# Later products with V, tiles of V grouped by head group, and the masked exponentials in two buffers (attention decode with a gated MLP, one core)

## The chip, the cores and the metric

The kernel runs on one core of a Trainium2 chip. The metric is the device time of one execution in microseconds (us). It is given as the median of several runs. Beside it there is one profiled execution, whose trace gives the start and the duration of every instruction and every DMA packet. All times of day in this text are us from the start of the profiled span.

## The reference

A decode step of eight sequences with one token each. Attention has 32 query heads and 8 key/value heads of 128, so four query heads share one key/value head, and it looks at the last 2048 positions of the cache:

```python
xn = layernorm(x)                                   # x: 8 x 1 x 512
q = (xn @ wq) split into 32 heads of 128
scores = q . k_cache[:, :, Sk-2048:] * 128**-0.5    # 8 kv heads
o = softmax(scores) @ v_cache[:, :, Sk-2048:]
s = o (8 x 4096) @ wo                               # -> 8 x 512
h = sigmoid(xn @ w_gate) * (xn @ w_up)              # 512 -> 1792
return x + s * silu(h @ w_down)
```

All inputs are bfloat16. What has to be read is the window of K (33.6 MB), the window of V (33.6 MB), `wq` and `wo` (4.2 MB each), and `w_gate`, `w_up` and `w_down` (1.8 MB each): 81.0 MB in all, all of it used once.

## The kernel before

**Tiles and rings.** All loads go through the queue of SyncE (SP), in one fixed order. `wq`, K and the three late weights share a ring of three buffers of 32 KB per partition (`KRING`); V has a ring of four buffers of 16 KB (`VRING`). K comes as eight tiles of 4.19 MB (K0 to K7), four for each *set* of four sequences; V as sixteen tiles of 2.10 MB (V0 to V15), one per sequence `b` and head group `gg` (four kv heads each), in the order of `divmod(i, NG)`: sequence after sequence, the two head groups of a sequence in turn. The order on the queue is `wq`, K0 to K6, V0, V1, K7, V2 to V13, `w_gate`, `w_up`, V14, V15, `w_down`, and `wo` in eight pieces.

**Slots.** The kernel is scheduled by hand: the loop at L651 runs over slots `t`, and each engine executes its instructions in the order in which the slots write them. A slot holds at most the following, in this order:

- L657 `soft_max_part`: a maximum on VectorE (DVE) over the scores of a K tile that is complete;
- L660 `soft_exp` at `EXP_AT` = 36 and 68: two small DVE instructions, then four Exp on ScalarE (ACT), L484, with the sum of each row;
- L663 `soft_mask`: four DVE instructions (L539) that multiply the transposed exponentials `pc_bf` of one head group with the four columns of a 0/1 mask, into `pT_sb`, the stationary operand of the products with V. `pT_sb` is one buffer for both head groups of a set (pool `work`, one buffer), and it is taken anew when `gg == 0`;
- L665 `k_turn(t)` for t < 64: a quarter of a half of a K tile is transposed in place on DVE (L441), eight of them per tile;
- L670 `soft_turn` (four DVE transposes, L504) one slot after `soft_exp`;
- L672 `qk(t - 4)`: four matmuls on TensorE (PE, L456) with what `k_turn(t - 4)` made;
- L674 `pv_sum`: once per V tile, the matmuls of L616 that add up a finished product, and the DVE scaling into `o_sb` (L625). They read `acc_sb`, which ACT copies out of PSUM (L606);
- L676 `pv(u)`: a quarter of a V tile's products (L595). After the fourth quarter ACT's copy L606 is written down;
- L679 `soft_spread` two slots after `soft_exp`: eight matmuls (L517) and four ACT casts (L525) that make `pc_bf`;
- L681 `soft_den`: the row sums and their reciprocals, on DVE, PE and DVE (L551 to L577).

**When a load is issued.** `issue_loads` (L198) issues the next load of the fixed order as soon as the buffer that it takes is free in the order of the program: K7 after `qk(39)` (slot 43) has let K4 go, V(i+4) after the fourth quarter of V(i). On the chip that is a wait of SP for the engine that read the buffer last. A load that waits holds up all those behind it on the queue.

**Where the products stand.** `PV_AT` says at which slot the products of a set begin: 49 for the first and 83 for the second (L64 to L67). V(i) of the first set has the slots 49 + 4i to 52 + 4i. `soft_mask` comes one or two slots ahead of `PV_AT`: slots 47 and 48, and 81 and 82. `soft_den` comes in slots 48 and 82. The products of the first set's tiles (`PV_WIDE`, i < 8) take four chunks of V per matmul, those of the second set two.

After the products come the MLP (L688 to L693, L696), the rearrangement of `o_sb` (L695), the product with `wo` (L702) and two small DVE instructions ahead of the store.

Of the kernel before, what the change touches and what calls it, by code (L numbers as in the profile page):

```python
# [10 lines left out]
def kernel(  # L11
# [14 lines left out]
    P = 128  # L26
# [3 lines left out]
    rep = Hq // Hkv  # L30
# [11 lines left out]
    GL = 4  # L42
    NG = Hkv // GL
    PP = P // GL
    CH = W // PP
    NQ = P // 32
    NJ = 4
    CC = CH // NJ
    NT = B * NG
    NSLOT = NT * NJ  # L50


    HB = B // NQ
# [7 lines left out]
    VSET = NT // HB  # L61
    QK_LAG = 4
    EXP_AT = [SET * (hb + 1) + QK_LAG for hb in range(HB)]
    PV_LAG = 13  # L64
    PV_AT = [EXP_AT[0] + PV_LAG]
    for hb in range(1, HB):
        PV_AT.append(max(EXP_AT[hb] + 5, PV_AT[hb - 1] + VSET * NJ + 2))  # L67


    NA = Dh // 64  # L70
    CB = CH // 2
# [6 lines left out]
    bf16 = mybir.dt.bfloat16  # L78
# [6 lines left out]

    consts = ctx.enter_context(tc.tile_pool(name="consts", bufs=1))
    work = ctx.enter_context(tc.tile_pool(name="work", bufs=1))
    small = ctx.enter_context(tc.tile_pool(name="small", bufs=2))
    kring = ctx.enter_context(tc.tile_pool(name="kring", bufs=KRING))
    vring = ctx.enter_context(tc.tile_pool(name="vring", bufs=VRING))  # L90
# [14 lines left out]
    def load(dst, src, q=None):  # L105
        if q is None:
            q = nc.sync
        q.dma_start(out=dst, in_=src)  # L108
# [4 lines left out]
    def v_tile(shape, name):  # L113
        return vring.tile(shape, bf16, name=name, tag="vring", align_bytes=ALIGN)
# [10 lines left out]
    def load_k(i):  # L125
# [8 lines left out]
        )  # L134
        k_tiles[i] = t

    def load_v(i):
        b, gg = divmod(i, NG)
        t = v_tile([P, CH, Dh], "v_sb")
        load(  # L140
            t[:].rearrange("p c d -> p (c d)"),
            A_v_cache[b, GL * gg : GL * (gg + 1), win0:Sk, :].rearrange(
                "j (p c) d -> p j (c d)", c=CH
            ),
        )
        v_tiles[i] = t
# [18 lines left out]
    def load_wo():  # L165
# [19 lines left out]
        (kind, i)  # L185
        for _, kind, i in sorted(
            [(KTS * i, 0, i) for i in range(NKT)]
            + [(NJ * (i % VSET) + PV_AT[i // VSET], 1, i) for i in range(NT)]
        )
    ]  # L190
    loads[-2:-2] = [(2, 0)]
# [6 lines left out]
    def issue_loads():  # L198
# [36 lines left out]
        out=rstd[:], in_=mv[:, 1:2], func=AF.Sqrt, bias=eps_t[:], scale=1.0  # L235
# [4 lines left out]
        out=xn_bf[:],  # L240
# [7 lines left out]
    for kt in range(KT):  # L248
        nc.tensor.transpose(
            out=xnT_ps[:, kt, :], in_=xn_bf[:B, kt::KT], identity=ident[:B, :B]  # L250
        )
    x2_ps = psum1.tile([NCOL * 32, DC], f32, name="x2_ps", tag="misc")
    for c in range(NCOL):
# [23 lines left out]
        out=PermF[:], in_=ident[:].rearrange("m (h q r) -> m q h r", q=NQ, r=rep)  # L277
# [4 lines left out]
        out=Hm[:],  # L282
# [7 lines left out]
    for j in range(GL):  # L290
        for gg in range(NG):
            g = NG * gg + j // 2
            nc.vector.tensor_copy(
                out=spread[:, gg, j % 2, :, j], in_=ident[:, 32 * g : 32 * g + PP]
# [3 lines left out]
    for w in (32, 64):  # L298
        rows_of = small.tile([P, w], f32, name=f"rows_of{w}")
        nc.vector.tensor_reduce(  # L300
            out=rows_of[:],
# [12 lines left out]
    for gg in range(NG):  # L314
        rows = slice(32 * gg, 32 * (gg + 1))
        cols = slice(NE * GL * rep * gg, NE * GL * rep * (gg + 1))
        for e in range(NE):
            nc.vector.tensor_copy(
                out=pick[rows, e, cols].rearrange("p (h d) -> p h d", d=NE)[:, :, e],
# [105 lines left out]
    pT_of = {}  # L425
# [7 lines left out]
    def k_turn(t):  # L433

        i, n = divmod(t, KTS)
        a, cq = divmod(n, 4)
        kw = k_tiles[i][:].rearrange("p c d -> p (c d)").bitcast(f32)
        kw = kw.rearrange("p (c a w) -> p c a w", a=NA, w=32)[
            :, KC4 * cq : KC4 * (cq + 1), a, :
        ]  # L440
        nc.vector.transpose(out=kw, in_=kw)  # L441
# [24 lines left out]
    def soft_max_part(i):  # L466
        hb, kq = divmod(i, NK)
        if kq == 0:
            mx_of[hb] = small.tile([P, NK], f32, name="mx")
        nc.vector.reduce_max(  # L470
            out=mx_of[hb][:, kq : kq + 1], in_=s_tiles[i][:], axis=AX.X
        )
# [24 lines left out]
    def soft_turn(hb):  # L497

        p_bf = p_of.pop(hb)[:].rearrange("p c k j o -> p (c k j o)")
        pt_of[hb] = ppool.tile([P, CH, PP], bf16, name="pt_bf", tag="pp")  # L500
        pt = pt_of[hb][:].rearrange("p c m -> p (c m)")
        w = CH * PP // 4
        for n in range(4):
            nc.vector.transpose(  # L504
                out=pt[:, w * n : w * (n + 1)], in_=p_bf[:, w * n : w * (n + 1)]
            )
# [23 lines left out]

    def soft_mask(hb, gg):

        if gg == 0:
            pT_of[hb] = work.tile(
                [P, NG, NQ * CB, GL, 2 * rep], bf16, name="pT_sb", tag="pT_sb"
            )
        pc = pc_of[hb][:, gg].rearrange("p q (c e) r -> p (q c) (e r)", e=2)
        for gl in range(GL):
            nc.vector.tensor_scalar(  # L539
                out=pT_of[hb][:, gg, :, gl, :],  # L540
                in0=pc,
                scalar1=Hm[:, gl : gl + 1],
                scalar2=None,
                op0=ALU.mult,
            )
# [34 lines left out]
    def pv(t):  # L580


        i, j = divmod(t, NJ)
        b, gg = divmod(i, NG)
        n_ch = 4 if i < PV_WIDE else 2
        w = 16 * n_ch
        if j == 0:
            acc_tiles[i] = psum_a.tile([P, n_ch * Dh], f32, name="acc_ps", tag="acc_ps")
        pT = pT_of[b // NQ][:, gg, CB * (b % NQ) : CB * (b % NQ + 1)].rearrange(
            "p c g n -> p (c g n)"  # L590
        )
        for n in range(CC // n_ch):
            c = n % (P // w)
            ch = CC * j + n_ch * n
            nc.tensor.matmul(  # L595
                acc_tiles[i][w * c : w * (c + 1), :],
                lhsT=pT[:, 16 * ch : 16 * ch + w],
                rhs=v_tiles[i][:, ch : ch + n_ch, :].rearrange("p c d -> p (c d)"),
                start=(j == 0 and n < P // w),
                stop=(j == NJ - 1 and n >= CC // n_ch - P // w),  # L600
                tile_position=(0, w * c),
                skip_group_check=True,
            )
        if j == NJ - 1:
            acc_sb = small.tile([P, n_ch * Dh], f32, name="acc_sb")
            nc.scalar.copy(out=acc_sb[:], in_=acc_tiles.pop(i)[:])  # L606
            acc_sbs[i] = acc_sb

    def pv_sum(i):
        b, gg = divmod(i, NG)  # L610
        n_ch = 4 if i < PV_WIDE else 2
        acc_sb = acc_sbs.pop(i)
        rows = slice(32 * gg, 32 * gg + GW)
        o_ps = psum1.tile([32 * NG, Dh], f32, name="o_ps", tag="misc")
        for c in range(n_ch):
            nc.tensor.matmul(  # L616
                o_ps[rows, :],
                lhsT=Sel[16 * n_ch][:, c].rearrange("p g r -> p (g r)"),
                rhs=acc_sb[:, Dh * c : Dh * (c + 1)],
                start=(c == 0),  # L620
                stop=(c == n_ch - 1),
                tile_position=(0, 32 * gg),
                skip_group_check=True,
            )
        nc.vector.tensor_scalar(  # L625
            out=o_sb[rows, b, :],
            in0=o_ps[rows, :],
            scalar1=rden_of[b // NQ][rows, b % NQ : b % NQ + 1],
            scalar2=None,
            op0=ALU.mult,  # L630
        )
# [16 lines left out]
        )  # L648

    KSLOT = NKT * KTS  # L650
    for t in range(PV_AT[-1] + VSET * NJ):  # L651
        u = -1
        for hb, at in enumerate(PV_AT):
            if 0 <= t - at < VSET * NJ:
                u = t - at + VSET * NJ * hb
        if QK_LAG + KTS <= t <= KSLOT + QK_LAG and (t - QK_LAG) % KTS == 0:
            soft_max_part((t - QK_LAG) // KTS - 1)  # L657
        for hb in range(HB):
            if t == EXP_AT[hb]:
                soft_exp(hb)  # L660
            for gg in range(NG):
                if t == PV_AT[hb] - NG + gg:
                    soft_mask(hb, gg)  # L663
        if t < KSLOT:
            k_turn(t)  # L665
        if t == 1:
            q_out(1, q_tiles[1], (0,))
        for hb in range(HB):
            if t == EXP_AT[hb] + 1:
                soft_turn(hb)  # L670
        if QK_LAG <= t < KSLOT + QK_LAG:
            qk(t - QK_LAG)  # L672
        if u >= NJ and u % NJ == 0:
            pv_sum(u // NJ - 1)  # L674
        if u >= 0:
            pv(u)  # L676
        for hb in range(HB):
            if t == EXP_AT[hb] + 2:
                soft_spread(hb)  # L679
            if t == PV_AT[hb] - 1:  # L680
                soft_den(hb)  # L681
        if t >= QK_LAG and (t - QK_LAG) % KTS == KTS - 1:
            released.add((0, (t - QK_LAG) // KTS))
        if u >= 0 and u % NJ == NJ - 1:
            released.add((1, u // NJ))
        issue_loads()
        if u == NSLOT - 2 * NJ - 1:
            unit_in(wgu_sb[0])  # L688
            unit_in(wgu_sb[1])
            released.add((2, 0))  # L690
            issue_loads()
        if u == NSLOT - 2 * NJ:
            unit_mid()  # L693
    pv_sum(NT - 1)
    o_rows()  # L695
    unit_out()  # L696
# [19 lines left out]
    for c in range(NCOL):  # L716
        queues[c].dma_start(
            out=out.flatten_outer_dims()[:, DC * c : DC * (c + 1)],
# [32 lines left out]
```

## Time and profile before

| what | value |
|---|---|
| runs | 198.0, 198.02 and 198.9 us; median 198.02 us |
| the profiled execution | 199.89 us, of which the span from the first to the last instruction is 198.1 us |
| busy share of the span | PE 50%, DVE 56%, ACT 15% |
| DMA | 81.16 MB in the span, mean 410 GB/s; queue of SP 96.4% of 16 engines' time |
| clock granted to TensorE, mean | 0.854 |

How it is read: the page of the profile gives the busy time of each engine, a row of tenths of the span cut in 40 slices, the groups of instructions by line, and the chain of work that ended last (from the last instruction back, at each step to what released it). The windows view gives the same for any stretch of time, with the DMA rate in its last column; a packet counts there where it starts. The timeline lists instructions in order of time; the bracket at its end says how long the engine had been idle and what ended that. "SPq" is SyncE's queue, that is, the moment at which a load is issued.

### The profile page before, as it was taken

How to read it: one execution, taken by the hardware profiler on the slowest of the kernel's cores; microseconds unless marked ns; L12 is line 12 of the kernel's file. 1: busy time of each engine (PE TensorE's matmuls, PEld its weight loads, DVE VectorE, ACT ScalarE, POOL GpSimd, SP SyncE). 2: the span in 40 equal slices, each digit the busy share in tenths (PEclk: the TensorE clock that was granted, in tenths of full speed). 3: DMA queues.
4: the chain of work that ended last, by engine and by line, in shares of the span. 5: the costliest groups of instructions: out<-in, count | busy, mean ns of one | idle time of the engine just before them, and what ended most of it. 6: DMA issues, size and time to landing. Idle time of an engine off the chain costs nothing.

```text
span 198.1 us, 2316 instructions
## 1 busy us (share of the span) xinstructions
PE 99.1 (50%) x950; PEld 43.9 (22%) x950; DVE 110.8 (56%) x182; ACT 29.1 (15%) x69; POOL 1.6 (1%) x8
## 2 busy tenths in 40 slices
PE   0133024434333039314986984888277633545693
PEld 0010001101011012001222331334045421223381
DVE  4706499999899969997995832501711100030301
ACT  3006050000000264000110115151101003000000
POOL 3000000000000000000000000000000000000000
PEclk9999999999999999855897999589958995555569
DMA  7999999999999999899999999999998999999990
GB/s 260 443 443 443 424 419 424 430 424 420 430 463 430 450 443 423 377 440 450 430 417 427 424 443 424 427 409 384 424 430 334 425 426 433 442 427 416 415 377 20
DMA packets 5242, 81.16 MB, mean 410 GB/s; under 512 B 600, under 2 KB 880, under 8 KB 1392
## 3 DMA queue, kind: packets, MB, share of 16 engines
q1 hardware_dynamic: 5200, 81.01, 96.4%
q8 instruction: 7, 0.11, 0.2%
q10 hardware_dynamic: 32, 0.01, 0.0%
q14 instruction: 3, 0.02, 0.0%
HBM read 81.01 MB, written 0.01 MB: 409 GB/s over the span
## 4 chain that ended last, share of the span: by engine, by line
DMA 53%; PE 20%; DVE 18%; ACT 6%; issue 2%; SPq 1%; ACTq 0%; DVEq 0%
DMA k_sb<-in_A_k_cache_dram 20%; DMA wd_sb<-in_B_w_down_dram 15%; DMA v_sb<-in_A_v_cache_dram 13%; DVE k_sb L441 12%; PE acc_ps L595 8%; PE o_ps L616 5%; DMA wo_sb<-in_A_wo_dram 5%; PE s_ps L456 3%; ACT p_bf L484 3%; PE pT_ps L517 2%; ACT acc_sb L606 2%; DVE pT_sb L539 2%; DVE pt_bf L504 1%; DVE mx L470 1%; SPq L108 1%
## 5 line engine op out<-in xcount | busy, mean ns | idle before, releaser
L441 DVE STREAM_TRANSPOSE k_sb<-k_sb 128x1024 f32<-128x1024 f32 x64 | 73.9, 1211 | 4.2 <-DMA k_sb<-in_A_k_cache_dram 4.1
L456 PE MATMUL s_ps<-k_sb,qz_sb 128*32 128x512 bf16 x256 | 29.3, 552 | 47.1 <-DVE k_sb L441 41.3
L595 PE MATMUL acc_ps<-v_sb,pT_sb 128*32 128x256 bf16 (+1 forms) x384 | 34.5, 371 | 9.2 <-DMA v_sb<-in_A_v_cache_dram 9.2
L625 DVE TENSOR_SCALAR o_sb<-o_ps,rden 16x128 bf16<-16x128 f32 x16 | 5.5, 341 | 49.3 <-PE o_ps L616 49.3
L456 PEld LDWEIGHTS <-qz_sb 128*32 128x32 bf16 x256 | 8.4, 114 | 70.7 <-issue 53.6
L616 PE MATMUL o_ps<-acc_sb,Sel 128*16 128x128 f32 x96 | 16.6, 321 | 10.5 <-ACT acc_sb L606 10.2
L606 ACT COPY acc_sb<-acc_ps 128x512 f32<-128x512 f32 (+1 forms) x16 | 7.7, 480 | 77.6 <-PE acc_ps L595 77.6
L595 PEld LDWEIGHTS <-pT_sb 128*32 128x32 bf16 (+1 forms) x384 | 14.4, 112 | 21.1 <-DMA v_sb<-in_A_v_cache_dram 9.0
L616 PEld LDWEIGHTS o_ps<-acc_sb,Sel 128*16 128x16 f32 x96 | 9.3, 109 | 18.0 <-ACT acc_sb L606 15.4
L517 PE MATMUL pT_ps<-pt_bf,spread 128*128 128x512 bf16 x16 | 6.7, 562 | 2.2 <-DVE pt_bf L504 2.0
L504 DVE STREAM_TRANSPOSE pt_bf<-p_bf 128x512 bf16<-128x512 bf16 x8 | 5.0, 680 | 4.8 <-ACT p_bf L484 4.8
L539 DVE TENSOR_SCALAR pT_sb<-pc_bf,Hm 128x1024 bf16<-128x1024 bf16 x16 | 6.5, 475 | 1.6 <-PE acc_ps L595 1.6
L470 DVE TENSOR_REDUCE mx<-s_ps 128x1 f32<-128x512 f32 x8 | 5.3, 667 | 3.6 <-PE s_ps L456 3.6
L382 PE MATMUL q_ps<-wq_sb,xnT_sb 128*32 128x512 bf16 x32 | 3.6, 630 | 7.3 <-DMA wq_sb<-in_A_wq_dram 7.3
L484 ACT ACT_TABLE_LOAD x1 | 1.3, 1283 | 39.7 <-DVE nm L478 39.7
L332 PE MATMUL d_ps<-wgu_sb,xnT_sb 128*32 128x448 bf16 x32 | 3.4, 573 | 5.7 <-DMA wgu_sb<-in_B_w_gate_dram 3.2
L484 ACT ACTIVATE p_bf<-s_ps,nm 128x512 bf16<-128x512 f32 x8 | 5.4, 686 | 4.0 <-DVE nm L478 4.0
L413 ACT COPY qz_sb<-qT_sb 32x32 bf16<-32x32 bf16 x20 | 4.8, 241 | 7.7 <-DVE qT_sb L401 7.5
L525 ACT CAST pc_bf<-pT_ps 128x512 bf16<-128x512 f32 x8 | 4.5, 587 | 8.9 <-PE pT_ps L517 6.3
L702 PE MATMUL a_ps<-wo_sb,o_sb 128*32 128x256 bf16 x64 | 5.2, 312 | 0.1
L568 PE MATMUL den_ps<-ones,dh 128*16 128x1 f32 x32 | 1.4, 166 | 6.9 <-DVE dh L555 6.4
L401 DVE STREAM_TRANSPOSE qT_sb<-q_sb 128x512 bf16<-128x512 bf16 x2 | 1.4, 690 | 6.3 <-ACT q_sb L396 6.3
(59 smaller groups left out, 42.2 us busy)
## 6 DMA issues: line engine op xcount, KB each, us to landing
k_sb<-in_A_k_cache_dram SPq DMA_DIRECT2D x8, 4096.0 KB, 21.9
v_sb<-in_A_v_cache_dram SPq DMA_DIRECT2D x16, 2048.0 KB, 17.9
wq_sb<-in_A_wq_dram SPq DMA_DIRECT2D x1, 4096.0 KB, 12.1
wo_sb<-in_A_wo_dram SPq DMA_DIRECT2D x2, 1024.0 KB
wgu_sb<-in_B_w_gate_dram SPq DMA_DIRECT2D x1, 1792.0 KB
wgu_sb<-in_B_w_up_dram SPq DMA_DIRECT2D x1, 1792.0 KB, 18.3
wd_sb<-in_B_w_down_dram SPq DMA_DIRECT2D x1, 1792.0 KB, 28.9
wo_sb<-in_A_wo_dram SPq DMA_DIRECT2D x3, 512.0 KB, 25.6
```

The costliest lines, as they stand in the source:

```text
L441: nc.vector.transpose(out=kw, in_=kw)
L456: nc.tensor.matmul(s_tiles[i][32 * g : 32 * (g + 1), :], lhsT=qz_sb[:, hb, h, 2 * a + e, :], rhs=kT[:, :, a, h, :, e], start=(n == 0), sto ...
L470: nc.vector.reduce_max(out=mx_of[hb][:, kq : kq + 1], in_=s_tiles[i][:], axis=AX.X)
L484: nc.scalar.activation(out=p_bf[:, :, kq], in_=s_tiles.pop(NK * hb + kq)[:].rearrange("p (o c j) -> p c j o", o=2, j=NC), func=AF.Exp, bia ...
L504: nc.vector.transpose(out=pt[:, w * n : w * (n + 1)], in_=p_bf[:, w * n : w * (n + 1)])
L517: nc.tensor.matmul(pT_ps[:], lhsT=spread[:, gg, y].rearrange("p k g -> p (k g)"), rhs=pt[:, c, y, :], start=(y == 0), stop=(y == 1), skip_ ...
L539: nc.vector.tensor_scalar(out=pT_of[hb][:, gg, :, gl, :], in0=pc, scalar1=Hm[:, gl : gl + 1], scalar2=None, op0=ALU.mult,)
L595: nc.tensor.matmul(acc_tiles[i][w * c : w * (c + 1), :], lhsT=pT[:, 16 * ch : 16 * ch + w], rhs=v_tiles[i][:, ch : ch + n_ch, :].rearrange ...
L606: nc.scalar.copy(out=acc_sb[:], in_=acc_tiles.pop(i)[:])
L616: nc.tensor.matmul(o_ps[rows, :], lhsT=Sel[16 * n_ch][:, c].rearrange("p g r -> p (g r)"), rhs=acc_sb[:, Dh * c : Dh * (c + 1)], start=(c ...
L625: nc.vector.tensor_scalar(out=o_sb[rows, b, :], in0=o_ps[rows, :], scalar1=rden_of[b // NQ][rows, b % NQ : b % NQ + 1], scalar2=None, op0= ...
L702: nc.tensor.matmul(a_ps[32 * c : 32 * (c + 1), :], lhsT=o2_sb[:, k, :], rhs=wo_parts[k][:, DC * c : DC * (c + 1)], start=(k == 0), stop=(k ...
```

## The change

Four things change together.

1. The products of all 16 V tiles stand in one row from slot 57 on (`PV_LAG`): V(i) has the slots 57 + 4i to 60 + 4i, for both sets. The first set's products thus begin eight slots later; the second set's begin at slot 89 in place of 83, without a break behind the first set's.
2. Within a set the tiles of V go by head group: V0 to V3 are the four sequences of head group 0, V4 to V7 those of head group 1 (`v_of`). The sizes, the number and the places of the loads on SP's queue stay as they were; only which slice of the cache a load reads differs.
3. `pT_sb` is now one buffer per head group, half as large, out of a pool with two of them (`work2`). So the mask of the second set's head group 0 may be written once V3's products are through, and that of head group 1 once V7's are.
4. `soft_mask` moves: first set to slots 39 and 40 (from 47 and 48), second set to slots 74 and 90 (from 81 and 82). `soft_den` moves to slots 41 and 73 (from 48 and 82).

```diff
-    PV_LAG = 13
-    PV_AT = [EXP_AT[0] + PV_LAG]
-    for hb in range(1, HB):
-        PV_AT.append(max(EXP_AT[hb] + 5, PV_AT[hb - 1] + VSET * NJ + 2))
+    V_LAG = 49
+    PV_LAG = 57
+    MASK_AT = {}
+    for gg in range(NG):
+        MASK_AT[0, gg] = EXP_AT[0] + 3 + gg
+        MASK_AT[1, gg] = PV_LAG + NJ * NQ * (gg + 1) + 1
...
+    work2 = ctx.enter_context(tc.tile_pool(name="work2", bufs=2))
...
+    def v_of(i):
+        hb, n = divmod(i, VSET)
+        gg, q = divmod(n, NQ)
+        return NQ * hb + q, gg
+
     def load_v(i):
-        b, gg = divmod(i, NG)
+        b, gg = v_of(i)
...
-            + [(NJ * (i % VSET) + PV_AT[i // VSET], 1, i) for i in range(NT)]
+            + [(NJ * i + V_LAG, 1, i) for i in range(NT)]
...
     def soft_mask(hb, gg):
-        if gg == 0:
-            pT_of[hb] = work.tile(
-                [P, NG, NQ * CB, GL, 2 * rep], bf16, name="pT_sb", tag="pT_sb"
-            )
+        pT_of[hb, gg] = work2.tile([P, NQ * CB, GL, 2 * rep], bf16, name="pT_sb")
...
-                out=pT_of[hb][:, gg, :, gl, :],
+                out=pT_of[hb, gg][:, :, gl, :],
...
     def pv(t):
         i, j = divmod(t, NJ)
-        b, gg = divmod(i, NG)
+        b, gg = v_of(i)
...
     def pv_sum(i):
-        b, gg = divmod(i, NG)
+        b, gg = v_of(i)
...
-    for t in range(PV_AT[-1] + VSET * NJ):
-        u = -1
-        for hb, at in enumerate(PV_AT):
-            if 0 <= t - at < VSET * NJ:
-                u = t - at + VSET * NJ * hb
+    for t in range(PV_LAG + NSLOT):
+        u = t - PV_LAG
...
-                if t == PV_AT[hb] - NG + gg:
+                if t == MASK_AT[hb, gg]:
                     soft_mask(hb, gg)
...
-            if t == PV_AT[hb] - 1:
+            if t == EXP_AT[hb] + 5:
                 soft_den(hb)
```

More of the change, by code (lines that the diff above doesn't have):

```diff
@@ L588, in pv @@
             acc_tiles[i] = psum_a.tile([P, n_ch * Dh], f32, name="acc_ps", tag="acc_ps")
-        pT = pT_of[b // NQ][:, gg, CB * (b % NQ) : CB * (b % NQ + 1)].rearrange(
-            "p c g n -> p (c g n)"
-        )
+        q = b % NQ
+        pT = pT_of[b // NQ, gg][:, CB * q : CB * (q + 1)].rearrange("p c g n -> p (c g n)")
         for n in range(CC // n_ch):
```

## The prediction

> **What bounds the kernel now.** I read the page first: its third part, the DMA row of the second, then the chain.
>
> ```profile
> DMA  7999999999999999899999999999998999999990
> ...
> q1 hardware_dynamic: 5200, 81.01, 96.4%
> ...
> DMA 53%; PE 20%; DVE 18%; ACT 6%; issue 2%; SPq 1%; ACTq 0%; DVEq 0%
> ```
>
> The loads fill the DMA engines nearly from end to end, and the chain runs over transfers. So only two things count: how long the stream stands still, and what follows its end (the last piece of `wo` lands at 194.61, the span ends at 198.1: 3.5 us that the change does not touch). The windows view shows where the stream is slow (the last column is GB/s):
>
> ```profile
> 24.00:82.00 58.00, 22.42 (x176) 6.75 (x179) 55.30 (x59) 9.31 (x25) 0.00 (x0) 1.00 1.00 432
> 82.00:131.00 49.00, 33.27 (x248) 11.50 (x240) 33.45 (x47) 6.88 (x16) 0.00 (x0) 0.76 1.01 432
> 131.00:142.00 11.00, 7.03 (x58) 3.40 (x56) 3.13 (x9) 2.63 (x5) 0.00 (x0) 1.00 0.95 387
> 142.00:148.00 6.00, 4.12 (x56) 2.72 (x56) 1.86 (x8) 0.00 (x0) 0.00 (x0) 0.64 1.01 434
> 148.00:157.00 9.00, 6.11 (x113) 4.05 (x112) 1.36 (x4) 1.49 (x4) 0.00 (x0) 0.86 0.96 383
> ```
>
> Full rate is 432 GB/s, one V tile each 4.85 us. The two dips cost 11 x 45/432 = 1.15 us and 9 x 49/432 = 1.0 us: **2.2 us** is all that a perfect order of the loads could win. The timeline of SP, ACT and DVE shows what made them:
>
> ```profile
> 121.10 0.69 ACT L484 ACTIVATE p_bf<-s_ps,nm 128x512 bf16<-128x512 f32 x1 [4.02 <-DVE nm L478]
> ...
> 123.77 0.60 ACT L606 COPY acc_sb<-acc_ps 128x512 f32<-128x512 f32 x1
> ```
>
> ```profile
> 132.27 0.54 SPq L108 DMA_DIRECT2D v_sb<-in_A_v_cache_dram  x1
> ```
>
> ```profile
> 139.56 3.26 DVE L539 TENSOR_SCALAR pT_sb<-pc_bf,Hm 128x1024 bf16<-128x1024 bf16 x8 [1.58 <-PE acc_ps L595]
> ```
>
> First dip: the second set's Exps begin at 121.10; V4's sum needs the ACT copy that stands behind them (123.77), and V5's products stand behind that sum and around the eight matmuls of the spread. V5 lets its buffer go at 132.27, when V9 is issued. Second dip: both masks wait for V7's last product (139.5), PE's products resume at 145.4, and V8 lets go only at 148.22, when V12 is issued.
>
> **How late a load may be.** Through V6 the queue carries 52.4 MB (`wq`, eight K, seven V). The windows give 394 GB/s over 0 to 24 and 432 after, so packets through V6 start until 123.5 and end, half a packet of 0.61 us later, at 123.8. One tile less or more is 4.85 us: V3 109.2, V4 114.1, V5 118.9, V8 133.5. In the packet records the first packet comes 1.35 us after the issue (V12: 149.55 after 148.22). So V4 must be issued by 107.9, V5 by 112.7, V6 by 117.6, V7 by 122.4. V9's limit was 132.1; issued 0.17 later it cost 1.15. A restart thus costs about 0.9 beyond the lateness: packets after it take about 1.0 us in place of 0.61.
>
> **The change, part by part.**
>
> *Mask and sums of set one earlier (slots 39 to 41).* K7 waits for `qk(39)`. PE now has the row sums' matmuls of slot 41 ahead of `qk(38)` and `qk(39)`, and these wait for DVE: from 74.85 four turns at 1.14, eight mask instructions in 3.3, 0.6 waiting for the first casts (76.6) give 83.3; sums and reciprocals took 1.8 (91.00 to 92.77), the `qk` 0.6 more: K7 is issued at about 85.8 in place of 79.52, V2 and V3 behind it. By the same count K7's bytes end at 99.4 and V1's a K tile (9.7) before, so the limit is 88.4: hidden, with 2.6 to spare; without that cover it costs the lateness and 0.9.
>
> *Products of set one eight slots later.* DVE goes on from 85.0 with fourteen turns and two maxima (0.6): 102.2. K7 landed at 101.42, so DVE does not wait. Then eight turns, a maximum and one scaling (0.34): 112.3, where before it was 115.40, because V2's products no longer hold `qk` up (106.31, 1.69 us on the DMA). PE starts V0 when turn 53 is done, about 100. At half clock a slot was 1.54 (94.48 to 96.00 and alike), at full clock four slots with a sum 4.75 (98.18 to 102.93). So V0's products end at about 105.3, V1's at 110.3, V2's at 115.0, and V4, V5, V6 are in time by 2.6, 2.4 and 2.6. In slot 67 `qk(63)` ends at about 114.2, then maximum and two small steps, 0.7 + 0.35: the Exps start at 115.1. DVE alone bounds this at 113.8 below; PE at half clock throughout gives 116.
>
> *What then stands behind the Exps.* The same list in the same order as before, with two tiles fewer behind it: ACT's copy for V2 behind the four Exps, V2's sum, two slots of V3's products, the spread, two slots more, and then V7 is issued. Before, the list took 132.27 - 121.10 = 11.2 us. But before, it held up V9; now V7, and the stream comes to V7 only 9.7 us earlier while the Exps come just 6.0 earlier. 11.2 of it were mostly at half clock. At full clock the sum takes 1.05, not 1.9; two slots 1.06, not 1.9; the spread about 2.4, not 3.1: 8.8. Bounds for V7's issue are 113.8 + 8.8 = 122.6 and 116 + 11.2 = 127.2. I take 125.8, near the half-clock row, since PE again idles over 3 us while the Exps run (115.0 to 118.3; before 120.9 to 124.4). Lateness 125.8 - 122.4 = 3.4, restart 0.9: **4.3 us lost** (1.1 to 5.7).
>
> On the clock: the granted clock was half from 123.2 to 130.0, after a stretch of 3.4 us (119.79 to 123.21) in which PE was busy 33%. The Trainium skill, "TensorE: Matmul & The Clock Gate", "What's actually happening", has it fall after an idle window of about 3.4 us and rise after a busy one. By that rule alone a gap of 3.3 us could leave the clock full; the sum would then be the third rival's. The row decides here: no window needed to be wholly idle.
>
> *V8.* V3's sum, four slots and, new here, set two's row sums in slot 73, whose PE matmuls wait for DVE (1.55 us from 142.73 to 144.28): 125.8 + 3.6 + 1.5 = 130.9. V7 ends at 127.2 + 0.9 + 4.85 = 132.9, so the limit is 131.6: just in time. V9 to V15 follow at 3.6 or less per tile against 4.85 of the stream, and gain on it.
>
> *Two mask buffers, head groups in turn.* The mask of group 0 (1.63) now stands in slot 74, behind V3, 15 slots before it is read; group 1 likewise in slot 90. The 6.0 us in which PE had no products (139.5 to 145.4) go, and so does the second dip, since V8's products follow V7's. What is late next there is the landing of the V tiles. The new order of V's slices moves the same sizes.
>
> **Sum.** 4.3 lost against 2.2: 2.1 longer. The profiled execution goes from a span of 198.1 to 200.2, and from 199.89 to 202.0; it lies 1.87 above the median of the runs, 198.02, so I carry the difference over to that: **200.1 us**.
>
> **Rivals.**
>
> 1. *A second standstill at V8* (0.16). Margin 0.7 us; PE at half clock through slots 69 to 76 adds 1.7, so V8 is 1.0 late and a restart comes on top: 2.0 more at most, about 1.3 likely, 201.3. The same time comes if the buffers do not do what is said and the masks still wait for V7: V12 is then late as before. For it: clock half after 123.2. Against: a busy window brought the clock back at 130.0, 5.6 us after PE resumed.
> 2. *The change does what its words say, and is faster* (0.10). One mechanism: the Exps start so early, and PE is so quick behind them, that V7 is issued by 122.4. Then the stream never stops and all 2.2 are won: 195.8. It decides at 122.4; my lower bound, 122.6, misses it by 0.2. For it: DVE's chain without V2's wait. Against: in slots 57 to 67 PE needs 1.2 a slot, as much as DVE, and starts at half clock.
> 3. *The clock stays full* (0.17). V7 is issued at 115.1 + 8.8 = 123.9, 1.5 late, 2.4 with the restart: 0.2 longer than before, 198.2. The rule of the Trainium skill above would allow this. For it: slots 57 to 68 keep PE busy. Against: the same gap before brought the half clock.
>
> The forecast itself has 0.57, from 199.1 to 201.2.
>
> **How the numbers follow.** No difference under 0.5% (1.0 us) can be told from none here. Slower: forecast and first rival, 0.73. Same: third rival, 0.17. Faster: second, 0.10. The range leaves out the second rival and the upper tail of the first, and takes in the lower bound of the loss (1.1 against 2.2: 197.0) in part: 197.4 to 201.9.
>
> For the DMA's start: "DMA: Bandwidth & Descriptors" of the Trainium skill, "Specifications", gives about 0.6 us to the first byte where the records show 1.35; by that figure, an estimate, V7 would be 0.7 less late and the sum 1.4 longer.
>
> **What would show it.** In the profile after: K7's issue near 86 without a dip; Exps at 115; no load between 115.5 and 125, V7's issue at 125 to 126.5; one dip in the DMA rate from about 124 to 128, deeper than both of before together; no dip between 142 and 157; PE waiting for V tiles from V8 on. I am wrong if V7 is issued before 123.5, if the rate dips a second time, or if K7, V4, V5 or V6 come after their limits.

## The result and the profile after

The changed kernel takes 205.11 us (median of 6 runs, 203.41 to 206.3) against 198.68 (median of 6, 198.0 to 199.76) for the kernel before: a ratio of 1.032, with a 95% interval from 1.0262 to 1.0377. Its profiled execution took 204.71 with a span of 202.9, so the two profiled executions differ by 4.8. The forecast, 200.1, had the direction right and was too small by 5; the range ended at 201.9. Ratios, here and below, are taken over those runs of a kernel that lie within 1.5% of its fastest, so they can differ a little from the quotient of the medians.

Two lines of the page of the kernel after, the DMA row in 40 slices of 5.07 us and the chain:

```profile
DMA  7999999999999999999999997499999999999990
...
DMA 45%; DVE 28%; PE 17%; ACT 6%; issue 2%; SPq 0%; ACTq 0%; DVEq 0%
```

There is now a hole in the row (7 and 4), and the chain runs 28% over DVE (18% before): followed back from V11's issue at 144.28, it goes through the products and the second set's Exps to the transposes of K ahead of the first products. The windows view of the kernel after (length, busy time and number of instructions of PE, PEld (PE's loads of its stationary operand), DVE, ACT and POOL, granted clock, DMA share, GB/s):

```profile
82.00:109.00 27.00, 13.73 (x112) 3.57 (x112) 25.92 (x29) 0.59 (x1) 0.00 (x0) 0.53 1.00 430
109.00:115.00 6.00, 5.22 (x46) 2.27 (x47) 3.17 (x4) 0.59 (x1) 0.00 (x0) 1.00 0.91 352
115.00:120.00 5.00, 3.23 (x29) 1.04 (x26) 1.34 (x4) 1.60 (x5) 0.00 (x0) 1.00 1.03 406
120.00:125.00 5.00, 3.28 (x16) 1.57 (x16) 2.77 (x5) 1.66 (x5) 0.00 (x0) 0.66 0.96 341
125.00:130.00 5.00, 4.03 (x26) 1.75 (x24) 0.00 (x0) 2.74 (x5) 0.00 (x0) 1.00 0.37 149
130.00:136.00 6.00, 4.74 (x52) 2.47 (x52) 3.05 (x10) 0.59 (x1) 0.00 (x0) 1.00 0.99 404
136.00:144.00 8.00, 6.53 (x58) 3.33 (x54) 0.69 (x2) 1.17 (x2) 0.00 (x0) 1.00 0.97 397
144.00:157.00 13.00, 7.19 (x120) 4.43 (x116) 3.04 (x8) 1.70 (x4) 0.00 (x0) 0.81 1.01 430
```

Against 432 GB/s the rows from 109 to 144 lose 1.1, 0.3, 1.05, 3.3, 0.4 and 0.65: 6.8 us. The dip near 149 is gone (430). The stream began to lose at 109, with V4, and not with V7 alone. The timeline shows why. PE at the first products:

```profile
102.26 1.04 PE L464 MATMUL s_ps<-k_sb,qz_sb 128*32 128x512 bf16 x8 [3.20 <-DVE k_sb L449]
103.23 1.06 PE L599 MATMUL acc_ps<-v_sb,pT_sb 128*64 128x512 bf16 x4
```

ACT at the second set's Exps and at the copy behind them, and SP's issues of V4 and V7:

```profile
118.40 0.69 ACT L492 ACTIVATE p_bf<-s_ps,nm 128x512 bf16<-128x512 f32 x1 [4.02 <-DVE nm L486]
...
121.07 0.60 ACT L610 COPY acc_sb<-acc_ps 128x512 f32<-128x512 f32 x1
```

```profile
108.40 0.54 SPq L111 DMA_DIRECT2D v_sb<-in_A_v_cache_dram  x1
```

```profile
128.47 0.54 SPq L111 DMA_DIRECT2D v_sb<-in_A_v_cache_dram  x1
```

V0's products began at 103.23, 3.2 us later than forecast, and V4 was issued at 108.40 (forecast 105.3). The Exps came at 118.40 (115.1) and V7 at 128.47 (125.8). PE and DVE between the last transposes and the Exps:

```profile
112.80 0.40 PE L464 MATMUL s_ps<-k_sb,qz_sb 128*32 128x512 bf16 x4 [0.39 <-DVE k_sb L449]
...
117.30 0.69 DVE L478 TENSOR_REDUCE mx<-s_ps 128x1 f32<-128x512 f32 x1 [1.44 <-PE s_ps L464]
```

### The profile page after: what moved, and what is told of

It is laid out like the page before. It is cut to its first block, busy times and chain, and to the rows that moved or that the text cites. A ratio compares the mean times of both kernels' runs of the same rounds, so it can differ in the third digit from the quotient of the medians.

```text
span 202.9 us, 2318 instructions
## 1 busy us (share of the span) xinstructions
PE 99.3 (49%) x950; PEld 44.2 (22%) x950; DVE 110.8 (55%) x182; ACT 29.0 (14%) x69; POOL 1.6 (1%) x8
## 4 chain that ended last, share of the span: by engine, by line
DMA 45%; DVE 28%; PE 17%; ACT 6%; issue 2%; SPq 0%; ACTq 0%; DVEq 0%
DVE k_sb L449 21%; DMA k_sb<-in_A_k_cache_dram 19%; DMA wd_sb<-in_B_w_down_dram 15%; PE acc_ps L599 8%; DMA v_sb<-in_A_v_cache_dram 6%; DMA wo_sb<-in_A_wo_dram 5%; PE o_ps L620 4%; PE s_ps L464 3%; ACT p_bf L492 2%; ACT acc_sb L610 2%; DVE pT_sb L544 2%; DVE mx L478 2%; PE pT_ps L525 1%; DVE pt_bf L512 1%; PE den_ps L573 1%
## 5 line engine op out<-in xcount | busy, mean ns | idle before, releaser
L464 PE MATMUL s_ps<-k_sb,qz_sb 128*32 128x512 bf16 x256 | 30.1, 583 | 51.7 <-DVE k_sb L449 45.9
L599 PE MATMUL acc_ps<-v_sb,pT_sb 128*32 128x256 bf16 (+1 forms) x384 | 32.5, 382 | 10.3 <-DMA v_sb<-in_A_v_cache_dram 10.3
L525 PE MATMUL pT_ps<-pt_bf,spread 128*128 128x512 bf16 x16 | 5.5, 477 | 2.3 <-DVE pt_bf L512 2.0
L703 PEld LDWEIGHTS <-o_sb 128*32 128x32 bf16 x64 | 4.2, 113 | 1.1 <-issue 0.6
```

The source lines that it names most:

```text
L464: nc.tensor.matmul(s_tiles[i][32 * g : 32 * (g + 1), :], lhsT=qz_sb[:, hb, h, 2 * a + e, :], rhs=kT[:, :, a, h, :, e], start=(n == 0), sto ...
L525: nc.tensor.matmul(pT_ps[:], lhsT=spread[:, gg, y].rearrange("p k g -> p (k g)"), rhs=pt[:, c, y, :], start=(y == 0), stop=(y == 1), skip_ ...
L599: nc.tensor.matmul(acc_tiles[i][w * c : w * (c + 1), :], lhsT=pT[:, 16 * ch : 16 * ch + w], rhs=v_tiles[i][:, ch : ch + n_ch, :].rearrange ...
L703: nc.tensor.matmul(a_ps[32 * c : 32 * (c + 1), :], lhsT=o2_sb[:, k, :], rhs=wo_parts[k][:, DC * c : DC * (c + 1)], start=(k == 0), stop=(k ...
```

## The experiments

A load's *turn* is the moment at which the tile ahead of it on the queue has ended, and its *lead* is how long before its turn it is issued; "turn 55", with a slot's number, is the transpose `k_turn(55)`.

**Theory A:** V4 to V7 are issued too late for the stream because the products that free their buffers stand later. **Rival B:** the new order of V's slices makes the transfers themselves slower. **Rival C:** the early masks and row sums, which delay K7, cost the time. The ratio is always to the kernel before on the same chip; that kernel's median was 199.29 (beside e1 to e4), 199.94 (e5 to e8) and 199.15 (e9 to e12), with single runs from 197.55 to 202.59.

| run | median us | ratio (95% interval) |
|---|---|---|
| e1 V by head group only | 198.64 | 0.9972 (0.9931 to 1.0012) |
| e2 early masks and sums only | 199.16 | 0.9989 (0.9942 to 1.0036) |
| e3 slot 57 only, loads resorted | 204.86 | 1.0278 (1.0218 to 1.0338) |
| e9 slot 57 only, loads as before | 207.04 | 1.0411 (1.0346 to 1.0476) |
| e4 changed, two weights ahead of V4 | 197.75 | 0.9926 (0.9898 to 0.9953) |
| e8 changed, two weights ahead of V7 | 201.23 | 1.0098 (1.0057 to 1.0139) |
| e11 changed, one weight ahead of V4 | 201.30 | 1.0126 (1.0072 to 1.0181) |
| e5 changed, slot 49 | 198.37 | 0.9976 (0.9933 to 1.002) |
| e6 changed, slot 53 | 201.31 | 1.0065 (1.0029 to 1.0102) |
| e7 changed, slot 55 | 203.91 | 1.0185 (1.0108 to 1.0262) |
| e10 before, two weights ahead of V9 | 197.87 | 0.9949 (0.9917 to 0.9982) |
| e12 changed, slot 49, two weights ahead of V8 | 197.65 | 0.9954 (0.9927 to 0.998) |

### One part of the change alone

**e1**, to the kernel before:

```diff
-        b, gg = divmod(i, NG)
+        b, gg = v_of(i)
```

> The kernel before with the tiles of V of a set by head group, and nothing else: slots, mask buffer, mask and sums as before. Theory A (V4 to V7 are issued too late because the products stand eight slots later): the order of the slices does nothing; same time as before within 0.5%, the two dips of the DMA rate at about 133 and 149 as before. Rival B (the new order of slices makes the transfers themselves slower): a tile takes longer than 4.85 us, packets slow down from about 109 on, and several of the 6 us are here: 201 or more.

No difference in time. Rival B falls. One thing came otherwise than expected: in this execution the first dip is missing (424 GB/s from 131 to 142). The Exps began at 119.71 in place of 121.10 and the list behind them took 10.6 us in place of 11.2, so V9 was issued at 130.28 in place of 132.27. So the first dip need not be in every execution.

**e2**, to the kernel before:

```diff
-                if t == PV_AT[hb] - NG + gg:
+                if t == (EXP_AT[0] + 3 + gg if hb == 0 else PV_AT[hb] - NG + gg):
...
-            if t == PV_AT[hb] - 1:
+            if t == (EXP_AT[0] + 5 if hb == 0 else PV_AT[hb] - 1):
```

> The kernel before with the first set's masks in slots 39 and 40 and its row sums in slot 41, as in the changed kernel, and nothing else. Theory A: K7 is issued near 85.7 in place of 79.5, hidden behind V1; same time as before within 0.5%. Rival C (the late issue of K7, V2 and V3, or what is queued behind the early masks, costs the time): a dip near 90, products later, 200 or more.

No difference, with K7 issued at 85.39 and 433 GB/s from 82 to 92: hidden. Rival C falls.

**e3**, to the kernel before:

```diff
-    PV_LAG = 13
+    PV_LAG = 21
```

> The kernel before with the first set's products in slots 57 to 88 and the second's from slot 91; order of V, one mask buffer and the early or late place of the masks relative to the products stay as before (masks in slots 55 and 56, sums in 56). Theory A: V0's first product waits for the transpose of slot 55 as in the changed kernel, so V0 starts near 103 to 104, V4 is issued near 108.5, V7 near 128 to 129, and the whole loss is here: 203 to 205.5. Rivals B and C: this part is harmless, 198 to 199.5.

As A expected in size, but not clean: the loads are sorted by `PV_AT`, so V0 and V1 moved behind K7, and K7 itself came late (332 GB/s from 76 to 84, 1.9 us lost). So it was run again as **e9**, with the loads' key fixed:

```diff
-    PV_LAG = 13
+    PV_LAG = 21
...
-            + [(NJ * (i % VSET) + PV_AT[i // VSET], 1, i) for i in range(NT)]
+            + [(NJ * i + 49, 1, i) for i in range(NT)]
```

> The third experiment again with the order of the loads on the queue as in the kernel before (there the sort had put V0 and V1 behind K7, and K7 itself came late and cost about 2 us): products of the first set from slot 57, of the second from 91, one mask buffer, V in the order before. Theory A: no dip near 80; V4 issued near 108 with 1.5 us to its turn, V7 near 128 after its turn: as slow as the changed kernel, 203 to 205. If the order of V by head group or the early masks add something to the lag, it comes out at 201 to 202.

A miss, above both ranges: the later products alone, with the masks and sums that stand right ahead of them, cost more than the whole change (207.04 against 205.11, in another batch). The windows of e9:

```profile
108.00:125.00 17.00, 12.42 (x100) 5.00 (x98) 9.49 (x15) 4.44 (x11) 0.00 (x0) 0.90 0.91 366
125.00:133.00 8.00, 7.32 (x42) 2.73 (x40) 0.34 (x1) 2.92 (x5) 0.00 (x0) 0.78 0.36 136
```

That is 2.6 and 5.5 us. Here masks and row sums stand in slots 55 and 56, right ahead of V0 (104.41), and V7 is issued at 130.45, 2.0 later than in the changed kernel. So the other parts of the change give back about 2 us of what the lag takes; which of them gives how much was not run.

### Loads that wait for no product, put in the gap

**e4**, to the changed kernel (e8 has 7 in place of 4):

```diff
-    loads[-2:-2] = [(2, 0)]
+    loads.insert(loads.index((1, 4)), (2, 0))
```

> The changed kernel with the loads of w_gate and w_up (8.5 us of the stream, into a K buffer free since about 97) moved on the queue from behind V13 to ahead of V4; all else as in the changed kernel. Theory A: the stream has 8.5 us of work that waits for no product, so V4 to V7 are no longer late (limits 116.4, 121.2, 126.1 and 130.9 against issues at 108.4, 113.8, 118.3 and 128.5): both dips go and the time falls to 195.5 to 197.5, below the kernel before. If the loss is anything but late loads of V (slower transfers, more work at the end), it stays above 201.

```profile
109.00:131.00 22.00, 16.45 (x118) 6.77 (x116) 7.65 (x14) 7.16 (x16) 0.00 (x0) 0.92 1.01 431
131.00:157.00 26.00, 17.22 (x220) 9.72 (x216) 6.40 (x19) 3.46 (x7) 0.00 (x0) 0.99 1.00 426
```

The windows of e4 show no dip, and with the products where the change put them the kernel is 0.7% faster than before. The median, 197.75, is a little above the expected 195.5 to 197.5; the reason is under "The base" in the next section. Loads put in like this are called cover below. So all that the change cost, 3.2% over the kernel before, hung on when loads were issued.

**e8**

> The changed kernel with the loads of w_gate and w_up ahead of V7 in place of V4. Theory A: the losses of V4 to V6 stay (by the windows of the changed kernel 1.1 us over 109 to 115, and more to 125), the gap ahead of V7 (3.3 us over 125 to 130) is filled: 3 to 4 us faster than the changed kernel, 199.5 to 202. If the small dips at V4 to V6 are only a shift that V7's wait would have taken up anyway, it falls as far as with the loads ahead of V4.

```profile
108.00:120.00 12.00, 9.08 (x80) 3.40 (x76) 5.44 (x9) 2.83 (x7) 0.00 (x0) 1.00 0.97 380
120.00:125.00 5.00, 3.34 (x17) 1.59 (x17) 2.76 (x5) 1.61 (x5) 0.00 (x0) 0.66 0.98 324
125.00:130.00 5.00, 4.03 (x26) 1.75 (x24) 0.00 (x0) 2.73 (x5) 0.00 (x0) 1.00 1.01 431
```

As A expected: V7's hole is filled (431 in place of 149), the losses of V4 to V6 stay (1.4 and 1.25).

**e11** splits the load of the two weights: `w_gate` ahead of V4, `w_up` (a kind of load of its own, 3) where both stood:

```diff
-    loads[-2:-2] = [(2, 0)]
+    loads[-2:-2] = [(3, 0)]
+    loads.insert(loads.index((1, 4)), (2, 0))
```

> The changed kernel with w_gate alone (4.25 us of the stream) ahead of V4, w_up where both stood. It sets the leads, that is, how long before its turn a load is issued: about 5.6 us for V4, 5.8 for V5, 6.7 for V6, 2.9 for V7. By the loads of the runs so far, a lead over 3.5 us costs 0 to 0.4 us and one of 1.3 to 3 us costs 0.4 to 1.6: nothing lost at V4 to V6, 0.5 to 1.5 at V7 though it is issued before its turn, 198.2 to 199.3. If only a load that comes after its turn cost something, it would be at the floor, 197.5 to 198.

A miss by 2, by my arithmetic: I had added 4.25 to V7's turn in the changed kernel, 127.1, in which the losses of V4 to V6 were still contained. With these covered V7's turn comes at 128.6, so V7, issued at 129.15, was late again. V4 to V6, issued 4.5 to 5.0 us ahead of their turn, cost 0 to 0.2. The windows of e11:

```profile
128.00:132.00 4.00, 3.06 (x29) 1.46 (x28) 0.69 (x3) 1.33 (x3) 0.00 (x0) 1.00 0.51 199
...
140.00:144.00 4.00, 3.27 (x31) 1.73 (x28) 0.34 (x1) 0.59 (x1) 0.00 (x0) 1.00 1.00 307
```

The second row is V9, issued 3.3 us *ahead* of its turn, and the DMA share is 1.00: by the packet records the 16 engines stood still for only 0.1 us each from 136 to 146, and most of V9's first 16 packets took 1.1 to 2.1 us in place of 0.61.

**e10** is e4's edit in the kernel before, ahead of V9:

```diff
-    loads[-2:-2] = [(2, 0)]
+    loads.insert(loads.index((1, 9)), (2, 0))
```

> The kernel before, with the loads of w_gate and w_up ahead of V9 on the queue in place of behind V13, and nothing else. Theory A: V9 (1.7 us ahead of its turn in the profile before) and V12 (1.5 us ahead) get 8.5 us more; no dip from 130 to 157; the time falls to the floor that the changed kernel with the loads ahead of V4 showed, 197.5 to 198.3, and spreads less than the kernel before. Rival: the dips only moved the waiting, and the end is set by something else: no change within 0.5%.

```profile
131.00:157.00 26.00, 15.83 (x190) 8.98 (x188) 5.72 (x18) 3.81 (x8) 0.00 (x0) 0.88 1.01 429
```

The windows of e10 have 429 where the kernel before had 396, and the ten runs lie within 197.69 to 198.09.

### Other places for the products

**e5**, **e6** and **e7** change one number of the changed kernel, to 49, 53 and 55; the second set's masks move along, but not ahead of slot 74:

```diff
-    PV_LAG = 57
+    PV_LAG = 53
...
-        MASK_AT[1, gg] = PV_LAG + NJ * NQ * (gg + 1) + 1
+        MASK_AT[1, gg] = max(PV_LAG + NJ * NQ * (gg + 1) + 1, EXP_AT[1] + 6)
```

> The changed kernel with the products from slot 49 on in place of 57 (the second set's first mask in slot 74, the second in 82); order of V, two mask buffers, early first masks as in the changed kernel. Theory A: as before V9 is the load behind the Exps, a dip of about 1.1 us near 133 stays; the wait of both masks for V7 is gone and with it the dip near 149: about 1 us faster than before, 197.0 to 198.0. Rivals B and C: like the changed kernel, over 201.

As expected in the profile: the first dip stays, the second is gone, so the two mask buffers, with V by head group, do what they are said to do. The median is 0.4 above the expected range, and the gain in time is within the interval. The windows of e5:

```profile
131.00:142.00 11.00, 8.21 (x98) 4.56 (x95) 3.27 (x11) 1.84 (x4) 0.00 (x0) 1.00 0.96 372
...
148.00:157.00 9.00, 4.13 (x52) 2.25 (x56) 0.68 (x2) 0.37 (x1) 0.00 (x0) 0.61 1.01 431
```

> The changed kernel with the products from slot 53 on (the second set's masks in slots 74 and 86). Theory A: V0 starts near 98 and V4 is issued near 104, V5 near 108, V6 near 113, V7 near 117.5 (limits 107.9, 112.7, 117.6, 122.4), V8 is the load behind the Exps and comes at about 126.5 against a limit of 127.2: the stream loses between nothing and 1.2 us, 196 to 198. If the loss grows evenly with the lag, it lies halfway between lags 49 and 57, near 201.

A miss by 3.3 us. V4 to V7 were in time (103.6, 109.0, 114.3, 118.9), but the Exps came at 119.0 (the prediction had them at 115.1 for the changed kernel), and V8 was issued at 129.2 in place of 126.5. The windows of e6:

```profile
128.00:132.00 4.00, 2.94 (x29) 1.39 (x28) 0.79 (x3) 1.30 (x3) 0.00 (x0) 1.00 0.52 211
...
140.00:144.00 4.00, 3.27 (x54) 2.06 (x50) 0.69 (x2) 0.58 (x1) 0.00 (x0) 1.00 0.92 311
```

Whatever the slot (49, 53, 55, 57), the Exps come at 120.2, 119.0, 119.9 and 118.4: after turn 63, at 112.8 to 114.5, PE still owes the scores of four slots, the products between them and a sum (in e7 the maximum also stands behind that sum's scaling). V0's products began at 93.9, 98.4, 99.0 and 103.2, so the Exps do not hang on them. The slot only chooses which load stands behind them: V9, V8, V8, V7.

> The changed kernel with the products from slot 55 on. It tells what the first products wait for. If a score matmul needs the transposes of the whole half tile (four turns), V0's first quarter runs at about 99, the second stops until turn 55 is done (102.2), and V4 is issued at about 107, only 1.5 us before that of the changed kernel; then V5 and V6 are on time, V7's products are split by the Exps and V7 comes at about 123 to 126, late by 1 to 3: 199 to 202. If it needed its own turn only, V4 would come 2.3 us (two slots) before.

Slower by 2 than the expected 199 to 202: V7 was issued at 120.37, in time, and the late load was V8, at 132.92 (196 GB/s from 128 to 136). But it settles what the first products wait for. PE in e7:

```profile
98.98 1.06 PE L599 MATMUL acc_ps<-v_sb,pT_sb 128*64 128x512 bf16 x4
102.26 0.62 PE L464 MATMUL s_ps<-k_sb,qz_sb 128*32 128x512 bf16 x4 [2.21 <-DVE k_sb L449]
102.80 1.06 PE L599 MATMUL acc_ps<-v_sb,pT_sb 128*64 128x512 bf16 x4
```

The first quarter runs at 98.98, then PE stops for `qk(52)` until turn 55 has ended, and V4 is issued at 106.74: 1.7 us ahead of the changed kernel. By the whole half tile it had to be about 1.5, by its own turn 2.3; the stop itself, 2.21 us on the DVE, is seen in the second line.

### The best version

**e12** joins slot 49 with e4's edit ahead of V8:

```diff
-    PV_LAG = 57
+    PV_LAG = 49
...
-    loads[-2:-2] = [(2, 0)]
+    loads.insert(loads.index((1, 8)), (2, 0))
```

> The changed kernel with the products from slot 49 on and w_gate and w_up ahead of V8. Theory A: all leads over 5 us, no dip, the floor again, 197.5 to 198.3: with the loads covered, neither the lag nor the head group order matters any more. Rival: the earlier products leave less at the end and it is faster than the floor by over 0.5 us.

At the floor and no lower. e4, e10 and e12 lie within 0.22 us of each other (197.75, 197.87, 197.65): with the loads covered, neither the slot (49 or 57) nor the order of V matters to the time.

## Why the prediction was wrong, step by step

**What held.** The kernel is as long as its stream, and the late load behind the Exps makes the hole. K7 was forecast at 85.8, hidden, and came at 85.67 without a dip. From the Exps to V7's issue: forecast 10.7 between bounds of 8.8 and 11.2, measured 128.47 - 118.40 = 10.1. The second dip is gone, and V8 was just in time (issued at 133.40, 1.7 before its turn).

**The step that failed: "PE starts V0 when turn 53 is done, about 100."** A score matmul of L456 reads from all four quarters of a half tile, and `k_turn` transposes one quarter: `qk(52)` to `qk(55)` all wait for turn 55. It stands in the code of `qk`, and the trace of before shows it, too: scores in groups of sixteen matmuls, one per four turns. I had followed one slot, one turn, and my sum used that twice.

```profile
33.20 1.90 PE L456 MATMUL s_ps<-k_sb,qz_sb 128*32 128x512 bf16 x16 [2.61 <-DVE k_sb L441]
37.71 1.90 PE L456 MATMUL s_ps<-k_sb,qz_sb 128*32 128x512 bf16 x16 [2.61 <-DVE k_sb L441]
```

The first time is at V0, which I had 3.2 us too early. V4, V5 and V6, "in time by 2.6, 2.4 and 2.6" in my sum, came 3.1, 3.5 and 3.3 us later than I had them: each past its limit.

The second time is at the Exps. "In slot 67 `qk(63)` ends at about 114.2" let the last four scores go one by one behind their own turns. Turn 63 ended at 112.75, near the 112.3 of my sum, but `qk(60)` to `qk(63)` all wait for it: by the lines shown above they begin at 112.80, have three slots' products and a sum between them, and the maximum starts at 117.30. So the Exps came 3.3 later and V7 2.7, at 128.47, past even my upper bound, 127.2. V0's late start is not the reason, for with V0 4 to 9 us earlier (e7, e6, e5) the Exps came no earlier.

V7's date gives the loss. By the prediction's own rule V7 at 128.47 against its limit of 122.4 is 6.1 late, 7.0 with the restart; 6.8 were lost, where I had 4.3.

**A price that I had left out: a load that comes near its limit.** I let a load be free until 1.35 us ahead of its turn. By the packet records (the end of a tile is here the mean end of its last 16 packets, as many as there are engines; the excess is what a tile took beyond 4.85 us):

```
kernel  load  lead us  excess us     kernel  load  lead us  excess us
e9      V7     -3.47     5.40        after   V6      2.67     1.30
after   V7     -1.38     3.14        e9      V8      3.21     0.06
e11     V7     -0.50     2.25        e11     V9      3.30     1.11
e6      V8      0.05     1.80        e6      V10     3.40     1.04
after   V4      1.24     0.97        e1      V9      3.62     0.11
after   V5      1.67     0.63        e4      V7      3.63     0.02
before  V9      1.81     0.74        after   V10     4.83     0.02
e5      V9      2.49     1.38        e11     V6      4.88     0.24
```

Over all loads from V2 on in the fourteen traces, 25 were issued 1.2 to 3.4 us ahead, and 22 of these cost 0.4 to 1.4; the 164 issued further ahead cost 0 to 0.4. V4, V5 and V6 thus cost 2.5 us (the windows from 109 to 125), which I had at nothing. But this does not explain the forecast's shortfall. V7 waits for products and not for these loads, so what they lost was taken out of its wait: it was issued 4.7 us after its turn in the undisturbed stream (123.8), and only 1.4 after its turn in the stream as it was (127.1). V7's own share, 3.4 and 0.9 in my sum, was 3.3 in its window and 1.05 in the two after it. Where V7 is covered, in e8, the losses of V4 to V6 stand alone, and there the price counts.

**The base.** I took 2.2 us of dips, read from one profiled execution, off a median that had hardly any of them. Without dips the floor is 197.65 to 197.87 (e4, e10, e12), so the first three runs of before, median 198.02, had lost 0.3, and the profiled one, 199.89, had lost 2.2. Over all batches the kernel before runs from 197.55 to 202.59, and e10, which differs only in that no load comes late, from 197.69 to 198.09: with the late loads goes nearly all of the spread. Three runs were too few, and they were lucky ones: in the later batches the median of the same kernel was 199.15 to 199.94, near the profiled execution. From the floor my own loss of 4.3 would have given 202.0; the measured 6.8 give 204.5, against 204.71 profiled. Of the 5.0 by which the forecast was too small, 2.5 are thus the loss, 1.9 the base, and 0.6 the distance from 204.5 to the median of the six runs. For the same reason the floor I gave e4 (195.5 to 197.5) was too low.

**The clock.** The list behind the Exps took 10.1 and not 11.2. The half clock lasted one step of 3.4 us there (121.2 to 124.6) in place of two (123.2 to 130.0 before), and the rows are shorter where it had ended: the two slots of products ahead of the spread took 1.58 in place of 1.92, the first half of the spread 1.04 in place of 1.89. The Trainium skill, "TensorE: Matmul & The Clock Gate", "What's actually happening", has it fall after an idle window of about 3.4 us. The trace agrees here, with PE busy 0.42 us in the 3.41 ahead of the fall (117.81 to 121.22), though before 33% of such a window did not keep it up.

**The rivals.** The first (a second standstill at V8, 201.3) did not happen: V8 came 1.7 ahead of its turn and cost 0.4. There were losses in another place, at V4 to V6, and they were no addition to V7's. The second and the third needed V7 by 122.4 or 123.9; with the Exps at 118.4 neither was near.

## What to carry to other kernels

When the stream of loads is the bound, write down for every load when it is issued and when its turn comes, and look for a lead (some 3.5 us here, for loads of 2.1 MB) at each, not for whether it is late; a load that depends on nothing belongs on the queue ahead of the ones that wait for buffers. When you date a matmul, read which columns its operand takes: it starts after the last instruction that writes any of them, whatever slot it is written in. When several loads in a row are late, do not add up their losses: the one that is latest against the undisturbed stream sets the sum. And find out how much of the profiled execution's loss the median shares before you take it off the median.

## What the hardware showed that I had not expected

After the stream had run dry, V7's first packet in the changed kernel started at 129.8, 1.3 us after the issue at 128.47 (also 1.3 for the late loads of e3, e7 and e9). "DMA: Bandwidth & Descriptors" of the Trainium skill, "Latency and other measured facts", has about 600 ns to the first byte on this path; the measurement decides.

A load that is issued in time but not long ahead slows the stream without a gap. V6 of the changed kernel was issued at 118.26, 2.7 us ahead of its turn at 120.9. The 16 engines stood still for only 0.1 us each from 118 to 122, but half of V6's first 16 packets took 1.1 to 2.4 us in place of 0.61. In e8, two more loads stood right behind V6 on the queue, and it cost 1.0 all the same. So a lack of further work alone does not explain it; what does, and why V8 of e9 (3.2 ahead) paid 0.06 and V9 of e11 (3.3 ahead) 1.11, no run here settles.
